# A Fourier-mix and attention kernel on Trainium2: products of zeros ahead of the first operands, and the first operands loaded, rounded and multiplied in another order

## The chip, the cores and the metric

The kernel runs on one core of one Trainium2 chip. The metric is the device time of one execution in microseconds (us). The kernel before takes 1727.77 us, the median of three runs (1727.48 to 1729.41).

The engines are named as the profile names them. PE multiplies matrices, and PEld is its load of the stationary operand. DVE is VectorE, ACT is ScalarE, POOL is GpSimd. SP is SyncE, which here only issues DMAs. SPq, ACTq and so on are the engines' instruction queues, where DMAs are issued.

## The reference

With x of 2048 rows and 512 columns, the kernel computes a gated sum of two branches:

```python
g = sigmoid((x * gate_w).sum(-1, keepdims=True))
# branch A: the real part of a DFT over columns, then rows
a, b = x @ Wd_re.T, x @ Wd_im.T
A = Ws_re @ a - Ws_im @ b
# branch B: attention, 32 heads of 16
q, k, v = split_heads(x @ wqkv)
B = (softmax(q @ k.T * 16 ** -0.5) @ v) @ wo
out = g * A + (1 - g) * B
```

All arrays are float32. The kernel writes each operand as a high part, rounded to the matrix engine's single-pass float format (fp32r in the profile), plus a low part, the remainder. A product of two operands is then three matrix products: high by high, low by high, high by low.

## The kernel before, in words

The kernel has two stretches. The first, about 200 us, makes q and k (the lines 127 to 187), v and the imaginary part of the column DFT (lines 286 to 342). The second, about 1500 us, weaves attention, the DFT over rows and the output projection into each other, in patterns written out by hand (lines 754 to 861). The order of instructions is fixed throughout: every engine and every DMA queue works its instructions in the order of the program, and each waits for its operands by semaphores.

The change touches the beginning and one small step near the end.

**The beginning.** x is held transposed: `xab[tb]` holds four blocks of 128 rows by 512 columns for the column block `tb` (512 of the 2048 positions), each as high and low part. `wh` and `wl` are the high and low parts of the weights of q (c = 0) and k (c = 1), in four parts `kt` of 128 input rows. `add` (line 98) puts a load on a list: first the weights of q and the x of `tb` 0, in turn for `kt` 0 to 3, so that load 0 is w of `kt` 0, load 1 is x of `kt` 0, load 2 is w of `kt` 1, load 3 is x of `kt` 1. Then come the weights of k, the x of `tb` 1 to 3, the weights of v and of the column DFT. `load_ahead` (line 101) issues loads of 256 KB each into one of six staging buffers `raw`, all from SP (line 95), five ahead. `split(n)` (line 106) takes n staged arrays in order. For each, `hi_lo` (line 74) rounds the high part on ACT (line 75) and subtracts it on DVE, for some on POOL (line 76), and the buffer is free for the next load.

`split(8)` (line 154) thus queues the rounding of all eight arrays of q's weights and the first x. The loop at line 173 then runs over `kt` and, within it, over the four tiles `ct` of 128 q rows. Each call of `mm_qk` issues the three products of one tile and one `kt` (lines 79 to 81): high by high, w high by x low, w low by x high. So four accumulators grow in turn, 48 products in all. Then `split(4)` queues the weights of k, and `evac_qk` (line 136) takes the four accumulators out, high part by ACT and low part by DVE, and SP writes them to memory. All other tiles of q and k are made one at a time, twelve products each, with one or two splits between a tile's products and its evacuation (lines 180 to 185). Their accumulators rotate through six banks, three named s and three named a.

**The step near the end.** The softmax denominators of four pairs of heads at a time are gathered into a tile `rc` of 128 rows by 64 (`sums`, line 476), inverted by DVE (`inverse`, line 484) and written back for a later multiplication. The last group of the second half of the rows has three pairs (n = 3), which leaves 32 of the 128 rows of `rc` unwritten, and there the inversion is done in two calls of 48 rows (line 491). `sums` and `inverse` of that group are placed by the plan at steps 482 and 484 of 512 (lines 721 to 726).

Of the kernel before, what the change touches and what calls it, by code (L numbers as in the profile page):

```python
# [9 lines left out]
F32 = mybir.dt.float32  # L10
F32R = mybir.dt.float32r
AF = mybir.ActivationFunctionType
ALU = mybir.AluOpType
AX = mybir.AxisListType

P = 128
# [5 lines left out]
KT = D // P  # L22
# [9 lines left out]
def mix_kernel(ctx: ExitStack, tc: tile.TileContext, xa_t, xa, wqkv, w_hid, w_seq, wo, gate_w, out):  # L32
# [5 lines left out]
    nc = tc.nc  # L38
# [5 lines left out]
    psD = ctx.enter_context(tc.tile_pool(name="psD", bufs=1, space=PSUM))  # L44
# [26 lines left out]
    xab = [const.tile([P, 4, 2, D], F32R, name=f"xab{tb}", tag=f"xab{tb}") for tb in range(4)]  # L71
    acc = psO.tile([P, 512], F32, name="acc")

    def hi_lo(hi, lo, src, lo_eng=None):
        nc.scalar.copy(hi, src)  # L75
        (lo_eng or nc.vector).tensor_tensor(lo, src, hi.bitcast(F32), ALU.subtract)

    def mm3(ps, sh, sl, mh, ml, first, last):
        nc.tensor.matmul(ps, sh, mh, start=first, stop=False)  # L79
        nc.tensor.matmul(ps, sh, ml, start=False, stop=False)  # L80
        nc.tensor.matmul(ps, sl, mh, start=False, stop=last)  # L81
# [8 lines left out]

    todo, loaded = [], []

    def staged(src):
        raw = st1.tile([P, D], F32, name="raw", bufs=RAW)
        nc.sync.dma_start(raw, src)
        return raw

    def add(hi, lo, src, lo_eng, shape=None):
        todo.append((hi, lo, src, lo_eng, shape))

    def load_ahead():
        while todo and len(loaded) < RAW - 1:
            hi, lo, src, lo_eng, shape = todo.pop(0)
            loaded.append((hi, lo, staged(src), lo_eng, shape))

    def split(n):

        for _ in range(n):
            load_ahead()
            if loaded:  # L110
                hi, lo, raw, lo_eng, shape = loaded.pop(0)
                hi_lo(hi, lo, raw.rearrange("p (s t) -> p s t", s=4) if shape else raw, lo_eng)
            load_ahead()

    def add_x(tb, kt):
        x = xab[tb][:, :, :, kt * P:(kt + 1) * P]
        add(x[:, :, 0], x[:, :, 1], xa_t[tb, :, kt], nc.vector, True)
# [3 lines left out]
    def bank():  # L121
        nonlocal banks
        banks += 1
        return (psS if banks % 2 else psA).tile([P, 512], F32, name="s" if banks % 2 else "a")


    with tc.tile_pool(name="qk", bufs=1, reuse_waits="tile") as pool:
        wh = pool.tile([P, 2, KT, D], F32R, name="wh")
        wl = pool.tile([P, 2, KT, D], F32R, name="wl")

        def mm_qk(ps, c, ct, tb, kt):
            cols = slice(ct * P, (ct + 1) * P)
            x = xab[tb][:, :, :, kt * P:(kt + 1) * P]
            mm3(ps, wh[:, c, kt, cols], wl[:, c, kt, cols], x[:, :, 0], x[:, :, 1], kt == 0, kt == KT - 1)

        def evac_qk(ps, c, ct, tb):
            hl = pool.tile([P, 2, D], F32R, name="hl", bufs=7)
            hi_lo(hl[:, 0], hl[:, 1], ps)
            nc.sync.dma_start(qk_d[c][:, ct * P:(ct + 1) * P, tb * 512:(tb + 1) * 512].rearrange("v p t -> p v t"),
                              hl.bitcast(F32))  # L140

        for kt in range(KT):
            add(wh[:, 0, kt], wl[:, 0, kt], wqkv[0, :, kt], nc.vector)
            add_x(0, kt)
        for kt in range(KT):
            add(wh[:, 1, kt], wl[:, 1, kt], wqkv[1, :, kt], nc.vector)
        for tb in range(1, 4):
            for kt in range(KT):
                add_x(tb, kt)
        for kt in range(KT):  # L150
            add(wv[0][kt], wv[1][kt], wqkv[2, :, kt], nc.gpsimd)
        for kt in range(KT):
            add(wch[:, kt], wcl[:, kt], w_hid[1, :, kt], nc.gpsimd)
        split(8)

        xgs = {}

        def gate_row(s):

            xg = xgs.pop(s)  # L160
            nc.vector.scalar_tensor_tensor(xg, xg, 1.0, gwb, op0=ALU.mult, op1=ALU.mult, accum_out=z[:, s:s + 1])
            if s + 5 < NT:
                xgs[s + 5] = staged(xa[s + 5])

        for tb in range(4):
            if tb == 2:
                assert not todo and not loaded
                nc.sync.dma_start(gwb, gate_w.broadcast_to([P, D]))
                xgs.update({s: staged(xa[s]) for s in range(5)})
            for c in range(2):  # L170
                if tb == 0 and c == 0:
                    pss = [bank() for _ in range(4)]
                    for kt in range(KT):
                        for ct in range(4):
                            mm_qk(pss[ct], c, ct, tb, kt)
                    split(4)
                    for ct in range(4):
                        evac_qk(pss[ct], c, ct, tb)
                    continue
                for ct in range(4):  # L180
                    ps = bank()
                    for kt in range(KT):
                        mm_qk(ps, c, ct, tb, kt)
                    split(1 if ct % 2 and tb else 2)
                    evac_qk(ps, c, ct, tb)
                    if tb > 1:
                        gate_row(8 * (tb - 2) + 4 * c + ct)
# [135 lines left out]
    for s in range(8):  # L323
        ps = psS.tile([P, 512], F32, name="s")
# [151 lines left out]
    def sums(hf, ct, n=4):  # L476

        rcs[hf, ct] = rc = work.tile([P, 64], F32, name="rc", bufs=2)
        for h in range(2):
            s0 = 32 if h else 16  # L480
            nc.sync.dma_start(rc[64 * h:64 * h + 16 * n],
                              o_d[hf][4 * ct:4 * ct + n, s0:s0 + 1].rearrange("p o (c f) -> (o c) p f", f=64))

    def inverse(hf, ct, n=4):
        rc = rcs.pop((hf, ct))
        if n == 4:
            nc.vector.reciprocal(rc, rc)
        for h in range(2):
            rows = rc[64 * h:64 * h + 16 * n]
            if n < 4:  # L490
                nc.vector.reciprocal(rows, rows)
            nc.sync.dma_start(r_d[hf][ct][h, :n].rearrange("p (c f) -> c p f", f=64), rows)

    def load_o(o, sm, hf, ct, q0, n=4):
# [226 lines left out]
    for hf in range(2):  # L721
        for ct in range(4):
            n = 3 if hf and ct == 3 else 4
            last = 32 * (4 * ct + n - 1) + 16 * (hf + 1)
            at(last + (4 if ct < 3 else 2), sums, hf, ct, n)
            at(last + (12 if ct < 3 else 4), inverse, hf, ct, n)
            if ct < 3:
                for half in range(2):
                    for step, du in enumerate((16, 20, 22)):
                        at(last + du + 8 * half, block, step, hf, ct, half)  # L730
# [167 lines left out]
```

## Time and profile before

| what | value |
|---|---|
| median of three runs | 1727.77 us |
| the profiled execution's own time | 1727.72 us |
| its span, from the first to the last instruction | 1725.9 us |
| time around the span | 1.8 us |
| PE busy | 1711.7 us (99% of the span), 13009 products |
| DVE busy | 1364.2 us (79%) |
| ACT busy | 1150.7 us (67%) |
| POOL busy | 447.3 us (26%) |

The busy share of PE is an upper bound: its products overlap, and their ends are modelled. What one product costs the chain is read from the distance between the starts of two products in a row. The page also shows the chain of work that ended last, followed back from the last instruction, and for each group of instructions the idle time before it with what ended it. In rows of the timeline the columns are the start in us, the duration in us, the engine, the line, the operation, output and inputs, the count, and in brackets the idle time before and what ended it. Rows of one line's instructions give the shortest, median and longest duration in ns.

### The profile page before, as it was taken

Reading aid. Unit: us, or ns where it says so; the run is one execution under the profiler, and the core shown is the slowest. Engines: PE = TensorE matmul, PEld = TensorE weight load, DVE = VectorE, ACT = ScalarE, POOL = GpSimd, SP = SyncE. Lnnn points to the kernel's source line nnn. Section 1 sums busy time; section 2 is a strip of 40 time slices with the busy share of each in tenths; the row PEclk is TensorE's granted clock in tenths of the full one; section 3 lists DMA queues with packets and bytes.
Section 4 is the critical chain, followed back from the end, with each engine's and each line's share of the span. In section 5 each row is a group of like instructions: output and inputs, shape, how many; then the busy total and the mean of one; then the engine's idle time right before and its main releaser. Section 6 shows DMA issues by size and latency. Waiting matters only on the chain.

```text
span 1725.9 us, 33460 instructions
## 1 busy us (share of the span) xinstructions
PE 1711.7 (99%) x13009; PEld 1049.2 (61%) x13009; DVE 1364.2 (79%) x2295; ACT 1150.7 (67%) x2257; POOL 447.3 (26%) x561
## 2 busy tenths in 40 slices
PE   8999999999999999999999999999999999999998
PEld 7888745456665666666656666666666666544443
DVE  5439788888888888888888888888888888899953
ACT  5212377776776777667776777677677777777776
POOL 0211122322222333222222343333232343200111
PEclk9999999999999999999999999999999999999999
DMA  8963500314141434314147535233142534560113
GB/s 284 335 150 134 155 7 3 55 35 78 56 75 45 84 98 96 72 38 81 38 93 246 104 106 107 63 64 67 45 86 63 124 99 94 177 151 18 39 28 129
DMA packets 82350, 164.82 MB, mean 95 GB/s; under 512 B 19712, under 2 KB 19968, under 8 KB 78352
## 3 DMA queue, kind: packets, MB, share of 16 engines
q1 hardware_dynamic: 77840, 162.30, 37.0%
q8 instruction: 102, 1.67, 0.4%
q0 software_dynamic: 4352, 0.39, 0.3%
q14 instruction: 56, 0.46, 0.1%
HBM read 107.47 MB, written 54.52 MB: 94 GB/s over the span
## 4 chain that ended last, share of the span: by engine, by line
PE 98%; ACT 1%; DVE 0%; DMA 0%; issue 0%; DVEq 0%; ACTq 0%
PE d L381 35%; PE acc L679 28%; PE a L216 12%; PE s L670 12%; PE s L295 3%; PE s L327 1%; PE d L295 1%; PE s L79 1%; PE s L80 1%; PE a L79 1%; PE a L80 1%; PE s L81 1%; PE a L81 1%; ACT pt L671 0%; PE a L381 0%; PE acc L216 0%
## 5 line engine op out<-in xcount | busy, mean ns | idle before, releaser
L218 DVE TENSOR_REDUCE mx<-a 128x1 f32<-128x512 f32 x2026 | 1245.8, 682 | 243.6 <-PE a L216 227.6
L671 ACT ACTIVATE pt<-s 128x512 f32<-128x512 f32 x2008 | 1024.2, 620 | 389.1 <-PE s L670 328.9
L216 PE MATMUL a<-ks,qs 48*128 48x512 f32 x2026 | 813.9, 416 | 0.7 <-DVE mx L218 0.7
L670 PE MATMUL s<-qs,ks 50*128 50x512 f32 x2008 | 769.7, 413 | 0.4 <-ACT pt L671 0.2
L381 PE MATMUL d<-xab,ch 64*128 64x512 f32 x2016 | 648.5, 396 | 0.0
L679 PE MATMUL acc<-pt,vt 128*17 128x512 f32 x4096 | 500.7, 596 | 0.0
L381 PEld LDWEIGHTS d<-xab,ch 64*128 64x128 f32 x2016 | 366.0, 184 | 126.0 <-DVE mx L218 60.4
L670 PEld LDWEIGHTS s<-qs,ks 50*128 50x128 f32 x2008 | 366.1, 184 | 110.0 <-ACT pt L671 32.4
L216 PEld LDWEIGHTS a<-ks,qs 48*128 48x128 f32 x2026 | 368.2, 185 | 67.3 <-DVE mx L218 40.6
L381 PE MATMUL d<-xab,cl 64*128 64x512 f32 x1008 | 399.4, 396 | 0.0
L381 PEld LDWEIGHTS d<-xab,cl 64*128 64x128 f32 x1008 | 185.5, 184 | 64.9 <-DVE mx L218 40.8
L365 POOL CAST ch<-craw 128x512 fp32r<-128x512 f32 x126 | 77.3, 614 | 555.5 <-PE d L381 205.6
L679 PEld LDWEIGHTS acc<-pt,vt 128*17 128x17 f32 x4096 | 90.6, 96 | 205.9 <-issue 205.8
L366 POOL TENSOR_TENSOR cl<-craw,ch 128x512 fp32r<-128x512 f32 x126 | 162.5, 1289 | 10.2
L239 POOL DMA_DIRECT2D qs<-mt x128 | 72.2, 569 | 157.8 <-DVE mt L235 149.6
L381 PE MATMUL d<-wre,xab 64*128 64x512 f32 (+1 forms) x348 | 93.8, 402 | 0.1
L381 PEld LDWEIGHTS d<-wre,xab 64*128 64x128 f32 (+1 forms) x348 | 60.0, 185 | 32.3 <-issue 23.6
L381 PE MATMUL d<-wo_hl,o_hl 64*128 64x512 f32 (+1 forms) x261 | 71.0, 397 | 0.0
L75 ACT CAST hl<-s 128x512 fp32r<-128x512 f32 x28 | 16.1, 587 | 62.9 <-PE s L295 31.2
L381 PEld LDWEIGHTS d<-wo_hl,o_hl 64*128 64x128 f32 (+1 forms) x261 | 47.2, 185 | 16.1 <-issue 11.7
L230 POOL CAST nhl<-nm 128x16 fp32r<-128x16 f32 x32 | 6.3, 197 | 161.6 <-DVE nm L227 161.6
L398 POOL CAST xab<-y 128x512 fp32r<-128x512 f32 x16 | 9.8, 612 | 129.7 <-ACT y L397 107.1
(132 smaller groups left out, 970.9 us busy)
## 6 DMA issues: line engine op xcount, KB each, us to landing
craw<-w_seq SPq DMA_DIRECT2D x128, 256.0 KB
qk<-hl SPq DMA_DIRECT2D x32, 512.0 KB
qs<-qk SPq DMA_DIRECT2D x96, 128.0 KB
ks<-qk SPq DMA_DIRECT2D x96, 128.0 KB
b<-hl SPq DMA_DIRECT2D x16, 512.0 KB
xab<-b SPq DMA_DIRECT2D x16, 512.0 KB
o<-oe SPq DMA_DIRECT2D x62, 128.0 KB
oh<-nh SPq DMA_DIRECT2D x12, 512.0 KB
```

Source lines behind the costliest of these rows:

```text
L79: nc.tensor.matmul(ps, sh, mh, start=first, stop=False)
L80: nc.tensor.matmul(ps, sh, ml, start=False, stop=False)
L216: nc.tensor.matmul(ps, qs[p % 2][r, qt * P:(qt + 1) * P], ks[p % 2][r, kb * 512:(kb + 1) * 512], start=True, stop=True)
L218: user = nc.vector.tensor_reduce(mx[p % 2][:, h, qt, kb:kb + 1], ps, AX.X, ALU.max)
L239: (nc.sync, nc.gpsimd)[h].dma_start(rows.rearrange("v (q b c) -> v b q c", q=8, b=4)[:, b], mt[hf][32 * b + h:32 * b + 32:2])
L295: i = nc.tensor.matmul(ps, st[r], mv[r], start=not half and not j, stop=half == 1 and j == 11)
L365: nc.gpsimd.tensor_copy(h1, raw)
L366: nc.gpsimd.tensor_tensor(l1, raw, h1.bitcast(F32), ALU.subtract)
L381: i = nc.tensor.matmul(self.ps, st[r], mv[r], start=not self.begun, stop=stop)
L670: nc.tensor.matmul(ps, ks[p % 2][rr, kt * P:(kt + 1) * P], qs[p % 2][rr, q0:q0 + 512], start=True, stop=True)
L671: return nc.scalar.activation(pts[u][:, 2 * qb + h], ps, AF.Exp, bias=0.0, scale=DH ** -0.5)
L679: nc.tensor.matmul(acc[32 * j:32 * j + 17], vt[:, kt, p, 16 * h:16 * h + 17], pt[:, j], start=kt == 0, stop=kt == NT - 1)
```

## The change

Five things are changed.

- `warm_up` fills the place of one later x block in `xab[3]` with zeros on DVE, and PE multiplies it by itself nine times into an accumulator that is not read. These nine products stand ahead of all other products.
- Loads 1 and 3, the first two x loads, are issued by ACT's queue and no longer by SP's.
- `split_first` does the first weights and the first x: ACT rounds w, DVE rounds x, then DVE makes both low parts. `split(8)` becomes `split(6)`.
- In the loop over `kt` the order inside one `kt` is by parts: the four tiles' products of high by high, then the four of w low by x high, then the four of w high by x low.
- In `sums` with n = 3, POOL fills `rc` with ones ahead of the gathering, and `inverse` inverts all 128 rows in one call, as the other groups do.

```diff
-    def staged(src):
+    def staged(src, queue=None):
         raw = st1.tile([P, D], F32, name="raw", bufs=RAW)
-        nc.sync.dma_start(raw, src)
+        (queue or nc.sync).dma_start(raw, src)
         return raw
...
+    loads = 0
+
     def load_ahead():
+        nonlocal loads
         while todo and len(loaded) < RAW - 1:
             hi, lo, src, lo_eng, shape = todo.pop(0)
-            loaded.append((hi, lo, staged(src), lo_eng, shape))
+
+            loaded.append((hi, lo, staged(src, nc.scalar if loads in (1, 3) else None), lo_eng, shape))
+            loads += 1
...
+    def split_first():
+
+        load_ahead()
+        (wh0, wl0, w_raw, _, _), (xh0, xl0, x_raw, _, _) = loaded.pop(0), loaded.pop(0)
+        x_raw = x_raw.rearrange("p (s t) -> p s t", s=4)
+        nc.scalar.copy(wh0, w_raw)
+        nc.vector.tensor_copy(xh0, x_raw)
+        nc.vector.tensor_tensor(wl0, w_raw, wh0.bitcast(F32), ALU.subtract)
+        nc.vector.tensor_tensor(xl0, x_raw, xh0.bitcast(F32), ALU.subtract)
+        load_ahead()
+
+    def warm_up():
+
+        zeros = xab[3][:, 0, 0]
+        nc.vector.memset(zeros.bitcast(F32), 0.0)
+        ps = psD.tile([P, 512], F32, name="d")
+        for i in range(9):
+            nc.tensor.matmul(ps, zeros[:, :P], zeros, start=True, stop=True)
...
-        split(8)
+        warm_up()
+        split_first()
+        split(6)
...
                     for kt in range(KT):
-                        for ct in range(4):
-                            mm_qk(pss[ct], c, ct, tb, kt)
+                        x = xab[tb][:, :, :, kt * P:(kt + 1) * P]
+                        for i, (w, v) in enumerate(((wh, 0), (wl, 0), (wh, 1))):
+                            for ct in range(4):
+                                nc.tensor.matmul(pss[ct], w[:, c, kt, ct * P:(ct + 1) * P], x[:, :, v],
+                                                 start=kt == 0 and i == 0, stop=kt == KT - 1 and i == 2)
...
         rcs[hf, ct] = rc = work.tile([P, 64], F32, name="rc", bufs=2)
+        if n < 4:
+            nc.gpsimd.memset(rc, 1.0)
...
         rc = rcs.pop((hf, ct))
-        if n == 4:
-            nc.vector.reciprocal(rc, rc)
+        nc.vector.reciprocal(rc, rc)
         for h in range(2):
             rows = rc[64 * h:64 * h + 16 * n]
-            if n < 4:
-                nc.vector.reciprocal(rows, rows)
             nc.sync.dma_start(r_d[hf][ct][h, :n].rearrange("p (c f) -> c p f", f=64), rows)
```

## The prediction

> **What bounds the kernel now.** I read the chain that ended last first, then the table of stages of the first 90 us, then the timeline of the first 20 us engine by engine, and last the places where the chain leaves PE.
>
> ```profile
> span 1725.9 us, 33460 instructions
> ...
> PE 98%; ACT 1%; DVE 0%; DMA 0%; issue 0%; DVEq 0%; ACTq 0%
> ```
>
> The chain is PE almost throughout, so what PE does earlier at the beginning is worth its full length, if nothing later holds it back. The stages (bounds and length in us, then busy us and count of PE, PEld, DVE, ACT and POOL, the granted clock, the DMA share and GB/s) split at the first product, at the thirteenth, at the first of the second weight matrix, and at 50:
>
> ```profile
> 5.78:11.36 5.58, 5.58 (x13) 4.09 (x13) 4.75 (x8) 3.71 (x6) 0.00 (x0) 1.00 0.88 289
> 11.36:19.54 8.18, 8.18 (x37) 6.76 (x36) 3.99 (x7) 4.14 (x7) 0.00 (x0) 1.00 0.66 211
> 19.54:50.00 30.46, 30.46 (x136) 25.23 (x135) 15.64 (x25) 16.12 (x31) 7.26 (x6) 1.00 1.04 338
> 50.00:90.00 40.00, 40.00 (x178) 33.14 (x177) 18.18 (x41) 9.79 (x17) 3.91 (x4) 1.00 0.96 322
> ```
>
> PE is never idle from 5.78 to 90. But of the 48 products of the first four tiles, 12 start in the first 5.58 us and 36 in the next 8.18, which is 0.227 each. The timeline shows why:
>
> ```profile
> 0.74 1.28 ACT L75 ACT_TABLE_LOAD   x1 [0.74 <-PEq L891]
> 0.75 0.39 SPq L95 DMA_DIRECT2D raw<-wqkv  x1
> 1.19 0.42 SPq L95 DMA_DIRECT2D raw<-xa_t  x1
> ...
> 4.47 0.62 ACT L75 CAST wh<-raw 128x512 fp32r<-128x512 f32 x1 [2.45 <-DMA raw<-wqkv]
> 5.11 0.62 ACT L75 CAST xab<-raw 128x512 fp32r<-128x512 f32 x1
> 5.12 0.69 DVE L76 TENSOR_TENSOR wl<-raw,wh 128x512 fp32r<-128x512 f32 x1 [5.12 <-ACT wh L75]
> 5.76 0.69 DVE L76 TENSOR_TENSOR xab<-raw,xab 128x512 fp32r<-128x512 f32 x1
> ...
> 5.78 0.80 PE L79 MATMUL s<-xab,wh 128*128 128x512 f32 x1 [5.78 <-ACT xab L75]
> ...
> 6.50 0.80 PE L80 MATMUL s<-xab,wh 128*128 128x512 f32 x1
> ...
> 7.09 0.63 PE L81 MATMUL s<-xab,wl 128*128 128x512 f32 x1
> ...
> 10.94 0.58 PE L81 MATMUL a<-xab,wl 128*128 128x512 f32 x1
> ...
> 11.36 0.39 PE L79 MATMUL s<-xab,wh 128*128 128x512 f32 x1
> ```
>
> From the third product (7.09) to the twelfth (10.94) the nine steps are 0.428 each; from 11.36 they are 0.227, with the same shapes and sources. That is PE at about half rate for its first 5.58 us. The granted clock reads 1.00 in both stages, so at the start that column does not show it; the distances do. Ahead of that PE waits for w, rounded by ACT, then for x, rounded by ACT after it; and the second product waits for x's low part (0.72 behind the first).
>
> **The change part by part.** *Clock.* The fill of zeros, the products behind it and the rounding of x on DVE have these nearest rows:
>
> ```profile
> L340 DVE MEMSET acc<- x1: 485/485/485, 197.1 to 197.1; 128x512 f32 x1
> ...
> L528 DVE CAST o_lno<-o_raw x1: 416/416/416, 1661.6 to 1661.6; 128x512 fp32r<-128x512 f32 x1
> ```
>
> DVE should start with the other engines at 0.74, so the zeros stand at 1.25 and PE starts at about 1.3. Nine products at 0.428 are 3.85 us: PE is done at 5.15 at the latest, ahead of the first operands. They cost nothing while that holds; each 0.1 us beyond the operands would cost 0.1. The first 12 real products then take 12 x 0.227 = 2.73 instead of 5.58, **2.85 less**. When the clock rises is bounded thus: at best before the operands come (no loss); at worst as late behind its first product as now, 5.58, that is at 6.9, so that 1.3 us of real products run at half rate and lose 0.47 of it, 0.6. I take 0.2, nearer to the first, because the 5.58 of now hold gaps that nine products in a row do not.
>
> *Start.* The first x goes by ACT's queue. If its issue stands ahead of the table load, it leaves at 0.74 instead of 1.19. But x and w then share the engines, and both of today's first two loads were there by 5.11: w lands between 4.47 and 5.11, x by 5.11. ACT's rounding of w (0.62) ends between 5.09 and 5.73, DVE's of x (0.42) by 5.53. The first product starts between 5.15 and 5.8; I take 5.6, nearer to the late end, since the same bytes must come. So the second queue and the second engine hardly move the start. The two issues on ACT, about 0.4 each by SP's rows, lie in the 2.45 us in which ACT waits; SP's other loads leave 0.46 or 0.93 earlier, behind the same bytes.
>
> *Low parts, order.* DVE makes w's low part at 5.75 to 6.44 and x's to 7.13. Four products of high by high from 5.6 end at 6.5, four more at 7.4: in the new order the low parts come in time, where now the second and third products waited. What is late next is `kt` 1:
>
> ```profile
> 5.84 0.33 SPq L95 DMA_DIRECT2D raw<-wqkv  x1
> 6.15 0.62 ACT L75 CAST wh<-raw 128x512 fp32r<-128x512 f32 x1 [0.43 <-DMA raw<-wqkv]
> ...
> 7.16 0.62 ACT L75 CAST xab<-raw 128x512 fp32r<-128x512 f32 x1 [0.39 <-DMA raw<-xa_t]
> ...
> 9.35 0.62 ACT L75 CAST wh<-raw 128x512 fp32r<-128x512 f32 x1 [0.23 <-DMA raw<-wqkv]
> ...
> 10.04 0.62 ACT L75 CAST xab<-raw 128x512 fp32r<-128x512 f32 x1
> ```
>
> Loads 2 and 3 share again, so I let both land at 7.16, today's landing of the second of them. ACT rounds w by 7.78 and x by 8.42; `kt` 1 can start at 8.47. `kt` 0 is done at 5.6 + 2.73 + 0.2 = 8.53. So the two meet, and the four tiles end at 8.53 + 8.18 = 16.71 against 19.54: **2.83**. The low parts of `kt` 1 (to 8.5 and 9.2) are wanted at 9.4 and 10.3.
>
> *What is queued behind.* Loads 6 and 7 (the w and x of `kt` 3) wait for the buffers that the first low parts free. They now leave at 6.44 and 7.13 instead of 5.84 and 6.47, so ACT's two rows at 9.35 and 10.04 move to about 10.0 and 10.7; the low part of x is there by 12.1, and PE wants `kt` 3 at 8.53 + 24 x 0.227 = 13.98. Covered by 1.9.
>
> *Does the gain survive?* From 19.54 to 90 the DMA engines are full (shares 1.04 and 0.96), and loads that are not early can hold ACT, behind which the evacuations stand:
>
> ```profile
> 27.48 0.39 PE L81 MATMUL s<-xab,wl 128*128 128x512 f32 x1
> ...
> 30.53 0.62 ACT L75 CAST xab<-raw 128x512 fp32r<-128x512 f32 x1 [4.24 <-DMA raw<-xa_t]
> 31.06 0.58 ACT L75 CAST hl<-s 128x512 fp32r<-128x512 f32 x1
> ```
>
> A tile whose last product starts at 27.48 is taken out at 31.06, since ACT waits 4.24 us for an x load. With PE 2.83 earlier and the loads not at all, that lag grows from 3.2 to 6.0, and with both halves of the evacuation (0.58 and 0.69) to 7.3. Six banks give five tiles of 12 x 0.227, 13.6 us. The cover holds, and everything behind is released by PE.
>
> *Reciprocals.* Here DVE is the bound for a moment:
>
> ```profile
> L491 DVE RECIPROCAL rc<-rc x2: 533/541/549, 1638.3 to 1638.9; 48x64 f32<-48x64 f32 x2
> ...
> L487 DVE RECIPROCAL rc<-rc x7: 506/508/552, 572.6 to 1680.6; 128x64 f32<-128x64 f32 x7
> ...
> 1638.37 0.45 DVE rc L491
> ...
> 1638.85 0.55 DVE rc L491
> ...
> 1640.18 0.50 PE L216 MATMUL a<-ks,qs 48*128 48x512 f32 x1 [0.69 <-DVE mx L218]
> ```
>
> Both calls stand in the chain (the third and fourth rows), and PE then waits 0.69 for DVE. One call of 0.51 in place of two, 1.08, frees **0.57**; the gain lies between nothing (if another wait takes its place) and 0.69. I take 0.57, because the wait is longer than what goes. The fill of ones runs on POOL:
>
> ```profile
> 1618.67 1.86 POOL L499 MEMSET o_raw<- 128x1024 f32 x2
> 1656.27 0.20 POOL L230 CAST nhl<-nm 128x16 fp32r<-128x16 f32 x1 [35.74 <-DVE nm L227]
> ```
>
> In program order it stands ahead of the first of these rows, under 0.93 by that row's mean for 16 times the elements, and POOL is idle for 35.74 behind them; it costs nothing. Without that cover SP's gathering would wait for it, and the inversion behind that.
>
> *Sum.* 2.83 + 0.57 = 3.40. Against the profiled execution's own 1727.72 (span 1725.9, 1.8 around it), 0.05 under the median shown: **1724.3**.
>
> **The rivals.** *The clock rises late* (1725.3). What counts may be a stretch of time that does not begin with the first product. The end of the trace has a hint:
>
> ```profile
> 1717.50:1718.00 0.50, 0.38 (x3) 0.06 (x1) 0.50 (x2) 0.22 (x1) 0.50 (x1) 1.00 0.29 107
> 1718.00:1718.50 0.50, 0.46 (x2) 0.46 (x4) 0.50 (x1) 0.47 (x1) 0.50 (x1) 0.51 0.56 217
> ```
>
> The clock falls to half at 1718.0 while products are still issued, so the decision has its own time. If it rises at 8.0, 2.4 us of real products lose 0.47 of it, 1.13: `kt` 0 ends at 9.46, the tiles at 17.64, 1.90 earlier, with the reciprocal 2.47. For it: now it took 5.58. Against: nine products fill 3.85 us without a gap. [...]
>
> *The products of zeros do not release the clock* (the change does not do what it says, 1726.5): the first 12 real products take 12 x 0.428 = 5.14 from 5.6, ending at 10.74, and the tiles end at 18.92, 0.62 earlier; with the reciprocal 1.19. Only that no product of zeros stands in this trace speaks for it.
>
> *x stands behind the table load* (1725.2): ACT issues it at 2.02. With the first load's 3.72 from issue to use it lands at 5.74, behind SP's loads as late as 7.16; in between, the first product starts at 6.7 and the tiles end at 17.6, 1.93 earlier. In the trace the table load is ACT's first instruction, but so is the activation behind it, so this stays open. [...]
>
> *More* (1723.7): x and w land early, the start is 5.15, `kt` 1 is ready at 7.8, and the head gives 3.48.
>
> *The reciprocal pays nothing* (1724.9): another wait of PE's or ACT's follows at once.
>
> *Slower* (1729.7): the second queue's first x waits behind full rings. The point from which it decides is a first product at 19.54 + 0.57 - 48 x 0.227 = 9.2, x landing at 8.75. Loads into full rings are that slow later on, as the tile of k's stacks shows:
>
> ```profile
> DMA to landing us min/median/max: 5.8/8.7/11.0
> ```
>
> From 2.02, 8.7 us give 10.7, a first product at 11.2 and tiles ending at 22.1, 2.56 later, less 0.57. Against it: at the start only three of SP's loads are in the rings.
>
> **How the numbers follow.** Chances: the forecast 0.50 (1723.9 to 1724.8), more 0.13, late clock 0.12, no clock 0.08, x behind the table load 0.08, no reciprocal 0.04, slower 0.05. The range 1723.2 to 1726.0 leaves out no clock and slower, and some of the edges. A measurement of this kernel can tell about 0.2%, 3.46 us, from no change, and the forecast, 3.4, sits right at that: half of its cases and all of "more" lie beyond. So faster by over 0.2% 0.43, within 0.2% 0.54, slower by over 0.2% 0.03.
>
> **What would show it.** Right: PE's first product of zeros at 1.3; distances of 0.227 from the first or second real product on; first product near 5.6; the first product of k's weights near 16.7; the later stages 2.8 earlier each, without a PE wait up to 90; one reciprocal at about 1635 and a PE wait near 0.1 behind it. Wrong: distances of 0.428 beyond 7; ACT's table load ahead of its DMA issues; a wait for `kt` 1 beyond 8.6; PE waits between 19 and 60.

## The result, and the profile after

The changed kernel takes 1725.33 us, the median of 20 executions (1724.36 to 1727.86). The kernel before, taken beside it in 20 executions, took 1728.43 (1727.15 to 1732.44). The ratio is 0.9982, with a 95% interval of 0.9976 to 0.9989: 0.18% or 3.10 us less, where 3.40 was forecast. As a time, 1725.33 is 1.03 above the 1724.3 of the forecast; 0.66 of that is that the kernel before came out at 1728.43 and not at the 1727.77 known when the forecast was made.

The profiled execution of the changed kernel is one of its longer ones: 1726.38, with a span of 1724.3, where the median span of the 20 is 1723.4. Against the profile before, the span is only 1.6 shorter. That a single pair of profiles differs from the medians shows how much varies from one execution to the next. These are the page's span and the shares of the chain:

```profile
span 1724.3 us, 33482 instructions
...
PE 98%; DVE 0%; DMA 0%; ACT 0%; issue 0%; POOL 0%; DVEq 0%; ACTq 0%; POOLq 0%
```

The table of stages (columns as before) at the first product of zeros, the first real product, the thirteenth and the first of k's weights:

```profile
1.46:5.61 4.15, 4.15 (x10) 2.87 (x10) 0.54 (x2) 1.90 (x2) 0.00 (x0) 1.00 0.84 272
5.61:9.19 3.58, 3.58 (x14) 2.89 (x13) 3.08 (x6) 2.18 (x4) 0.00 (x0) 1.00 0.74 258
9.19:17.35 8.16, 8.16 (x37) 6.76 (x36) 4.70 (x7) 4.21 (x7) 0.00 (x0) 1.00 0.86 280
```

The first 12 real products take 3.58 (5.58 before), the other 36 take 8.16 (8.18 before), and the first product of k's weights starts at 17.35 (19.54 before). The head has given 2.19. The timeline of the changed kernel's head:

```profile
0.74 0.90 ACTq L95 DMA_DIRECT2D raw<-xa_t  x2
0.75 1.34 SPq L95 DMA_DIRECT2D raw<-wqkv  x3
0.92 0.48 DVE L134 MEMSET xab<- 128x512 f32 x1 [0.92 <-PEq L919]
...
1.46 4.21 PE L137 MATMUL d<-xab 128*128 128x512 f32 x9 [1.46 <-DVE xab L134]
1.67 1.28 ACT L125 ACT_TABLE_LOAD   x1 [1.67 <-PEq L919]
...
4.84 0.62 ACT L125 CAST wh<-raw 128x512 fp32r<-128x512 f32 x1 [1.89 <-DMA raw<-wqkv]
5.03 0.43 DVE L126 CAST xab<-raw 128x512 fp32r<-128x512 f32 x1 [3.63 <-DMA raw<-xa_t]
...
5.61 0.77 PE L203 MATMUL s<-xab,wh 128*128 128x512 f32 x1
...
6.17 0.63 PE L203 MATMUL a<-xab,wh 128*128 128x512 f32 x1
...
6.63 0.62 ACT L75 CAST wh<-raw 128x512 fp32r<-128x512 f32 x1 [1.17 <-DMA raw<-wqkv]
...
7.03 0.47 PE L203 MATMUL a<-xab,wh 128*128 128x512 f32 x1
...
7.16 0.62 ACT L75 CAST xab<-raw 128x512 fp32r<-128x512 f32 x1
...
7.33 0.40 PE L203 MATMUL s<-xab,wl 128*128 128x512 f32 x1
```

ACT's two DMA issues stand ahead of its table load. The products of zeros run from 1.46. The first real product comes at 5.61, and only behind the fourth, between 7.03 and 7.33, do the distances fall from 0.43 to 0.23. The trace's own record of the clock begins with its rise, here at 7.17 and in the kernel before at 11.35; that is why the column of the granted clock read 1.00 from the start.

Matching the n-th exponential of ACT in one trace with the n-th in the other shows where the rest went. The changed kernel is 2.13 ahead when the second stretch starts (197), 1.79 ahead at 1452 by many small steps, only 0.55 ahead behind 1486, 1.32 behind 1641, and 1.60 behind 1680. The step at 1486 is one wait of PE's:

```profile
1478.88 2.57 SPq L494 DMA_DIRECT2D wo_hl<-wo  x4
...
1480.07 0.56 POOL L268 DMA_DIRECT2D qs<-mt  x1 [2.64 <-issue]
...
1485.34 0.47 PE L698 MATMUL s<-qs,ks 50*128 50x512 f32 x1 [1.23 <-DMA qs<-mt]
...
DMA to landing us min/median/max: 1.7/1.7/5.1
```

SP issues the load of the output projection's weights, four transfers of 512 KB. POOL issues the last of eight DMAs that put a pair's row maxima beside q; it moves 2 KB and lands 5.1 us later, where the median of its kind is 1.7 (the last line, from the tile of the maxima). In the kernel before the longest was 3.9, and PE did not wait:

```profile
DMA to landing us min/median/max: 1.7/1.7/3.9
```

The step near 1641 is the reciprocal:

```profile
1637.80 0.54 DVE L517 RECIPROCAL rc<-rc 128x64 f32<-128x64 f32 x1
...
1638.94 0.50 PE L245 MATMUL a<-ks,qs 48*128 48x512 f32 x1
```

One call stands where two stood, and the PE product that waited 0.69 for DVE has no wait any more.

### The profile page after: what moved, and what is told of

It is laid out like the page before. It is cut to its first block, busy times and chain, and to the rows that moved or that the text cites. A ratio compares the mean times of both kernels' runs of the same rounds, so it can differ in the third digit from the quotient of the medians.

```text
span 1724.3 us, 33482 instructions
## 1 busy us (share of the span) xinstructions
PE 1713.2 (99%) x13018; PEld 1043.1 (60%) x13018; DVE 1364.3 (79%) x2296; ACT 1149.4 (67%) x2256; POOL 446.5 (26%) x562
## 4 chain that ended last, share of the span: by engine, by line
PE 98%; DVE 0%; DMA 0%; ACT 0%; issue 0%; POOL 0%; DVEq 0%; ACTq 0%; POOLq 0%
PE d L410 35%; PE acc L707 28%; PE a L245 12%; PE s L698 12%; PE s L324 3%; PE s L356 1%; PE d L324 1%; PE a L81 1%; PE a L79 1%; PE s L81 1%; PE s L79 1%; PE a L80 1%; PE s L80 1%; PE a L410 0%; PE s L203 0%; PE a L203 0%
```

## The experiments

The theory to test was that all of the head's gain comes from the products of zeros, because they bring the clock up sooner (the clock theory). The rival was that the second queue, the rounding on two engines and the order by parts carry a good part (the operands theory). A second question was what sets the time of the rise. The executions of one kernel differ by more than the small terms (1724.36 to 1727.86 for the changed kernel), so these are read from the traces, and the times stand beside them. "Rest" below is the time from the first real product to the first of k's weights, less 48 products at the fast distance (8.16 / 36 each, from the stages above) and less 0.47 of the stretch at half rate (the share that a distance of 0.428 loses against 0.227): what PE waited in the head.

| run | first real product | clock rises | first of k's weights | rest |
|---|---|---|---|---|
| before | 5.78 | 11.35 | 19.54 | 0.27 |
| changed | 5.61 | 7.17 | 17.35 | 0.13 |
| b_warm | 5.81 | 4.49 | 17.32 | 0.63 |
| a_nowarm | 5.89 | 11.79 | 19.62 | 0.07 |
| b_recip | 5.55 | 10.20 | 18.88 | 0.26 |
| a_onequeue | 5.51 | 6.47 | 16.94 | 0.10 |
| a_again | 5.74 | 7.37 | 17.52 | 0.13 |
| a_four | 5.52 | 11.52 | 19.33 | 0.11 |
| a_order | 5.49 | 4.54 | 17.52 | 1.16 |
| a_late_wo | 5.46 | 4.29 | 16.46 | 0.12 |
| c_best | 5.49 | 6.12 | 16.74 | 0.07 |
| b_late_wo | 5.86 | 10.03 | 18.99 | 0.29 |
| c_z8 | 5.72 | 10.64 | 19.01 | 0.10 |
| c_z7 | 5.84 | 5.08 | 16.81 | 0.09 |

**The products of zeros alone (b_warm)**, added to the kernel before:

```diff
+        warm_up()
         split(8)
```

> The kernel before plus the fill of zeros and the nine products of zeros, nothing else. Clock theory (all that the head gains comes from the products of zeros): first product of zeros at about 1.5, half rate until about 7.1, the first product of k's weights at 17.4 instead of 19.54, and the time 2.1 lower. Operands theory (the second queue, the rounding on two engines and the order by parts carry a good part): the second and third real products still wait for the low parts, the first product of k's weights comes at 17.9 or later, and the time is 1.6 lower or less.

The first product of k's weights came at 17.32, as early as in the changed kernel. PE's rows of this run:

```profile
1.46 3.74 PE L121 MATMUL d<-xab 128*128 128x512 f32 x9 [1.46 <-DVE xab L118]
5.81 0.50 PE L79 MATMUL s<-xab,wh 128*128 128x512 f32 x1 [0.60 <-ACT xab L75]
6.53 0.50 PE L80 MATMUL s<-xab,wh 128*128 128x512 f32 x1 [0.23 <-DVE xab L76]
```

But it got there in another way than expected. The clock rose at 4.49, while the zeros were still running, so no real product ran at half rate, and 0.63 was lost to waiting for low parts. With the changed kernel's later rise it would have come about 0.6 later: (7.17 - 5.81) x 0.47. The time, 1726.68 against 1727.21 (ratio 0.9998, 0.9988 to 1.0007), does not show the 2.1 that the clock theory expected; the span's median over 10 executions is 1724.35 against 1725.4, half of it. In the trace the lead is 2.16 at the start of the second stretch and 1.80 near the end. Why the median of the spans shows less is not known; of the time, a longer part around the span takes some more (up to 2.79 here, at most 1.85 in the kernel before beside it).

**Everything but the products of zeros (a_nowarm)**:

```diff
-        warm_up()
         split_first()
```

> The changed kernel without the fill and the products of zeros. Clock theory: first product near 5.6, half rate for 5.6 us behind it, so to 11.2, and the first product of k's weights at 19.1, 0.4 earlier than in the kernel before; the time is 1.8 over the changed kernel. Operands theory: the first product of k's weights at 18.5 or earlier.

The first product of k's weights came at 19.62, no earlier than in the kernel before. The clock rose at 11.79:

```profile
11.58 0.50 PE L194 MATMUL a<-xab,wh 128*128 128x512 f32 x1
11.91 0.39 PE L194 MATMUL s<-xab,wh 128*128 128x512 f32 x1
12.14 0.39 PE L194 MATMUL a<-xab,wh 128*128 128x512 f32 x1
```

So without the zeros the other three parts of the head bring little, and the clock theory holds against its rival as put. They do save 0.2 of waiting even so (a rest of 0.07 against 0.27); that it does not show at 19.62 is chance, since here the clock rose 5.90 behind the first product and in the kernel before 5.57. The time was 1726.0 against 1727.21 (0.9993, 0.9983 to 1.0002), about what the reciprocal alone gives below.

**The reciprocal alone (b_recip)**, on the kernel before:

```diff
+        if n < 4:
+            nc.gpsimd.memset(rc, 1.0)
...
-        if n == 4:
-            nc.vector.reciprocal(rc, rc)
+        nc.vector.reciprocal(rc, rc)
...
-            if n < 4:
-                nc.vector.reciprocal(rows, rows)
```

> The kernel before with the one change at the reciprocal (ones into the tile on POOL, one call of 128 rows). If DVE is the bound there: PE's wait of 0.69 at 1640 goes and the steps behind it come 0.6 to 0.8 earlier relative to those ahead; the time is 0.6 to 0.8 lower. Rival (another wait follows at once): the steps behind 1650 come less than 0.2 earlier.

From the 1930th to the 1960th exponential of ACT it took 21.61, against 22.44 in all three kernels with the old one (before, b_warm, b_late_wo) and 21.61 to 21.63 in every other with the new one: 0.83 less, somewhat over the 0.6 to 0.8 expected. The time was 1726.2 against 1727.21 (0.9995, 0.9986 to 1.0005). The wait does not come back; another 0.3 is gained behind 1680 in every kernel with this change whose clock did not fall there, and its cause stays open. The profile of this run shows something else, in three stages of 3.41:

```profile
1655.43:1658.84 3.41, 3.19 (x15) 1.71 (x12) 0.43 (x2) 2.87 (x7) 2.91 (x4) 1.00 0.01 1
1658.84:1662.25 3.41, 3.41 (x11) 2.17 (x9) 0.56 (x1) 1.20 (x3) 2.07 (x4) 0.50 0.04 4
1662.25:1665.66 3.41, 3.41 (x27) 1.18 (x24) 2.25 (x5) 2.81 (x6) 0.00 (x0) 1.00 0.00 0
```

In the middle of the kernel the granted clock fell to 0.50 for 3.41 us, behind a stage with 15 products, and rose again. It cost this execution 1.8 in its last part (55.60 from the 1960th exponential to the last one, against 53.75). It begins 1648.64 behind the rise (10.20 to 1658.84); the fall at the end comes 1706.66 behind it in the kernel before (11.35 to 1718.01) and 1710.08 in the changed one (7.17 to 1717.25), and what sets these times is not shown. The trace of b_late_wo below has the same fall, at 1658.67: its granted clock is 0.93 in the mean from 1650 to 1660 and 0.89 from 1655 to 1670. The granted clock listed for single executions hints that it is not rare: both of these list 0.997, and so do 17 of the 31 executions of the kernel before that ran beside a_again, but only 1 of the 20 of the changed kernel and none of the 10 of a_again. Whether all these hold such a fall is not shown.

**All first loads on one queue (a_onequeue)**:

```diff
-            loaded.append((hi, lo, staged(src, nc.scalar if loads in (1, 3) else None), lo_eng, shape))
+            loaded.append((hi, lo, staged(src, None), lo_eng, shape))
```

> The changed kernel with all first loads on SP's queue. If the second queue brings nothing: w lands at 4.47 again and x by 5.1, x is rounded by 5.55, and the first real product starts at 5.6 as in the changed kernel, the first product of k's weights at 17.3 to 17.4. If the second queue does bring x earlier: the first real product starts at 5.9 or later.

The roundings of the first two arrays:

```profile
3.96 0.62 ACT L125 CAST wh<-raw 128x512 fp32r<-128x512 f32 x1 [1.93 <-DMA raw<-wqkv]
...
4.93 0.43 DVE L126 CAST xab<-raw 128x512 fp32r<-128x512 f32 x1 [3.53 <-DMA raw<-xa_t]
```

w came 0.88 earlier than with two queues (3.96 against 4.84), x 0.10 earlier (4.93 against 5.03), and the first real product started at 5.51 against 5.61. With the second queue w comes later and x no earlier, so it brings nothing. The first product of k's weights came at 16.94 and not at 17.3, because the clock rose at 6.47. This kernel ran once, in 1724.9. In all runs the first product lies between 5.46 and 5.89 with two queues and between 5.49 and 5.86 with one.

**The changed kernel once more (a_again)**, without an edit:

> The changed kernel once more, unchanged, to see what varies between executions. [...] Delay theory (a fixed time behind the first product): the rise comes at 7.0 to 7.2 again. PE's wait for the DMA of the maxima's rows near 1484 is anything from 0 to 1.3.

The rise came at 7.37 instead of 7.17, and PE waited 0.7 near 1484. The time was 1725.47 against 1728.1 (0.9985, 0.9976 to 0.9994). This run alone does not speak against the delay theory, for 5.91 behind the first product of zeros is near the 5.71 of the first profile. The others do: with nine products from 1.46 the rise came at 4.29, 4.49, 4.54, 6.47, 7.17 and 7.37, that is 2.83 to 5.91 behind the first. The delay theory falls; what sets the rise within that spread is not shown.

**Four products (a_four)**:

```diff
-        for i in range(9):
+        for i in range(4):
```

> The changed kernel with four products of zeros instead of nine; they end at about 3.4, and PE is idle for 2.2 us until the first operands. [...] Rival (what counts is the sum of work since the start): the rise between 7.2 and 8.2, and the first product of k's weights by 17.7.

The rise came at 11.52 and the first product of k's weights at 19.33, so four products are as good as none. PE stood idle in front of the first real product, by the list of waits:

```profile
PE s L203 <- ACT wh L125: 2.0, 1, 2.0
```

It is not work summed up that counts: behind the idle 2.0 the rise came 6.00 after the first real product, about as late as without any zeros (5.57 in the kernel before, 5.90 in a_nowarm), and the rival, which had it by 8.2, falls. The time was 1727.55, 2.1 over a_again on the same chip, against 1.8 in the head.

**The old order inside a part (a_order)**:

```diff
-                        x = xab[tb][:, :, :, kt * P:(kt + 1) * P]
-                        for i, (w, v) in enumerate(((wh, 0), (wl, 0), (wh, 1))):
-                            for ct in range(4):
-                                nc.tensor.matmul(pss[ct], w[:, c, kt, ct * P:(ct + 1) * P], x[:, :, v],
-                                                 start=kt == 0 and i == 0, stop=kt == KT - 1 and i == 2)
+                        for ct in range(4):
+                            mm_qk(pss[ct], c, ct, tb, kt)
```

> The changed kernel with the old order inside each part kt, so that the second product wants the low part of x at once. The time from the first real product to the first of k's weights, less 48 products of 0.227 and less 0.47 of the stretch at half rate, is what PE waits: 0.13 in the changed kernel, 0.63 in the kernel before with the products of zeros. If the order by parts is what makes the difference: 0.5 to 0.8 here. If the rounding on two engines makes it: 0.2 or less.

The second product wants the low part of x, which DVE now makes after the high part of x and the low part of w:

```profile
5.49 0.47 PE L79 MATMUL s<-xab,wh 128*128 128x512 f32 x1 [0.27 <-ACT wh L125]
6.73 0.50 PE L80 MATMUL s<-xab,wh 128*128 128x512 f32 x1 [0.78 <-DVE xab L128]
```

The rest is 1.16, more than expected and more than the 0.63 of the old rounding with the old order. So once the clock is early and the rounding is shared, the order by parts is worth about 1.0, and the shared rounding without it loses 0.5. What the order is worth with the old rounding was not run. A part of the operands theory comes back here: these parts are worth 0.2 without the zeros and 0.5 beside them (0.63 in b_warm against 0.12). The time was 1726.41 against 1728.1 (0.9993, 0.9983 to 1.0003), 0.9 over a_again on the same chip.

**The later load (a_late_wo)**, a further edit on the changed kernel:

```diff
-            end_tiles(s // 4)
+            for i in ([], [0, 1], [2], [3])[s // 4]:
+                end_tiles(i)
```

> The changed kernel with the load of the output projection's weights (four of 512 KB on SP's queue, from 1478.9) issued one step later, together with the next loads near 1491; they are first used at 1507. If this transfer is what holds up the last DMA of the maxima's rows on POOL's queue: that DMA lands in about 1.7 us, PE's wait of 1.2 near 1484 is gone in every profile, and the time is 0.5 to 1.0 lower than the changed kernel's. Rival (that DMA is late by itself, by the 2.6 us that POOL stops ahead of issuing it): the wait stays between 0 and 1.3.

PE did not wait near 1484, and the longest landing of its kind was:

```profile
DMA to landing us min/median/max: 1.7/1.7/2.8
```

The DMA that had taken 5.1 took 1.69, though POOL stopped for 2.63 ahead of it as before; the rival falls. So it is in every trace: that DMA takes 1.69 to 1.73 in the five with the later load (c_best, c_z8 and c_z7 below among them) and 3.84 to 5.20 in the nine without. The time was 1724.47 against 1728.1 (0.9981, 0.9972 to 0.9991), 1.0 under a_again on the same chip. The same edit on the kernel before:

> The kernel before with the later load of the output projection's weights alone. If the wait for the DMA of the maxima's rows strikes the kernel before as often as the changed one, the time is 0.4 to 0.8 lower; if it strikes only the changed kernel, no change.

The time was 1727.57 against 1728.1 (0.9997, 0.9988 to 1.0006), and its profile has no such wait, but the fall of the clock near 1660 instead. By the time this is inconclusive. That the wait strikes kernels with the old head too is shown by b_recip, where it was 1.3.

**The best version (c_best)**, with the later load, one queue, and earlier and longer zeros:

```diff
-        zeros = xab[3][:, 0, 0]
+        zeros = xab[3][:, 0, 0, :P]
...
-        for i in range(9):
-            nc.tensor.matmul(ps, zeros[:, :P], zeros, start=True, stop=True)
+        for i in range(10):
+            nc.tensor.matmul(ps, zeros, zeros.rearrange("p (a b) -> p a b", a=1).broadcast_to([P, 4, P]), start=True, stop=True)
```

> The changed kernel with three edits: all first loads on SP's queue; the zeros filled over 128 columns instead of 512, read four times by each of now ten products; the load of the output projection's weights issued one step later. [...] The time is 3.5 to 4.5 under the kernel before, about that of the changed kernel with the late load or up to 0.3 lower.

PE started at 1.06, and the clock rose at 6.12. The spans of its 11 executions lie between 1722.1 and 1723.4, their median 1722.5 against 1726.3 before. The time was 1724.55 against 1728.1 (0.9981, 0.9972 to 0.9990). By its median it is under the kernel before and the changed one, but not under a_late_wo, which ran on another chip. The time gained 3.55 where the span gained 3.8, since the time around the span was 1.74 to 3.80 in this kernel. One line of the DMA table for the last 11 us of its profile, an execution with 2.9 around its span, is not there in the kernel before:

```profile
q8 instruction: 1, 0.02, 0.8%
```

One more block of instructions is fetched at the very end (103 in the trace instead of 102), and it starts at 1724.33, behind the span of 1722.6. To see whether fewer PE instructions avoid it, the same kernel ran with eight and with seven products:

```diff
-        for i in range(10):
+        for i in range(8):
```

> The kernel with the three further edits (one queue for the first loads, zeros over 128 columns, the late load of the projection's weights) with eight products of zeros instead of ten. Instruction theory (the time around the span grows to as much as 3.8 where the added PE instructions, two for each product, make one more block of instructions be fetched at the very end): eight products are 16 instructions, less than the 18 of the kernels in which it grew and more than the 8 of the one in which it did not, so it may go either way. [...]

> The same with seven products of zeros (14 instructions). Instruction theory: nearer to the 8 instructions that cost nothing, the time around the span 1.73 to 1.86 in every run, and the time 0.3 or so lower than with ten products, if the clock still rises in time. [...] Rival (the longer time around the span comes with the early clock and not with instructions): it is as scattered here as with ten.

The time around the span was 1.72 to 2.11 with eight and 1.73 to 2.84 with seven, and both profiles have the 103rd fetch. So the expectation that seven products cost nothing fell. In all, the time around the span is 1.73 to 1.86 in every execution with at most four products and up to 3.80 with seven or more. That it is the fetch is suspected, not shown: the four profiles with the 103rd fetch (b_warm, c_best, c_z8, c_z7) have 1.9 to 2.9 around their spans, but the profile of the changed kernel has 102 fetches and 2.1. The rival, that it goes with the early clock, is not shown either: three of the six executions with the longer span in c_z8, in which the clock seems to have risen late, have 1.89 to 1.99. The clock rose at 5.08 in the profile with seven products and only at 10.64 in the one with eight. The spans fall into two groups, 1722.2 to 1722.3 and 1724.0 to 1724.3 with eight, 1722.0 to 1722.4 and 1724.2 to 1724.9 with seven. The times were 1725.88 (0.9984, 0.9975 to 0.9993) and 1724.83 (0.9985, 0.9976 to 0.9994), each against 1727.42. Ten products, from 1.06, show no second group of spans in 11 executions.

## Why the prediction was right, and where it was off

The direction and the main mechanism were right: PE runs at about half rate at its start (distances of 0.43 against 0.23), products of zeros move that stretch ahead of the operands, and the gain passes through to the end. Step by step:

- *Zeros from 1.3, done by 5.15, ahead of the operands.* They ran from 1.46, since DVE started at 0.92 and not 0.74, and the last started at 5.03. The cover held but was thinner than thought.
- *The start, 5.6.* 5.61. That the second queue and the second engine hardly move it was right, and a_onequeue shows it for the queue. For the engine no run changes it alone; over all traces the first real product lies at 5.55 to 5.86 with x rounded by ACT and at 5.46 to 5.89 with x rounded by DVE.
- *The clock, 0.2, at worst 0.6.* This is the term that was mis-sized. Real products ran at half rate from 5.61 to 7.17 and lost 0.73, beyond the stated worst case. That bound, "as late behind its first product as now", took one execution's delay for a limit. The delay behind the first product of zeros was 2.83 to 5.91 in the nine-product runs. The rival "late clock" had the time of the rise rightly free of the first product, but it was kept as a separate case when it is a spread within every case. Its rise at 8.0 was the author's estimate and no run with nine products shows it; they showed 4.29 to 7.37.
- *`kt` 1 ready at 8.47.* It was ready at 7.78, since w had landed by 6.63 and x by 7.16, and ACT rounded each at once. It held nothing up.
- *The head, 2.83.* 2.19 in the first pair of profiles. The head before moves with its rise too: its first product of k's weights lay at 18.88, 18.99 and 19.54 in three traces, with the rise at 10.20, 10.03 and 11.35. The low parts came in time, as forecast, because of the order by parts.
- *The gain survives 20 to 90.* It did: PE has no wait there in the changed kernel.
- *The reciprocal, 0.57.* 0.83, and 0.3 behind it, so it was beyond the 0.69 given as its most. The distance between the product that waited and the one ahead of it fell from 1.08 (1639.10 to 1640.18 in the kernel before) to 0.35 (1638.59 to 1638.94), which is 0.73; where the last 0.1 and the later 0.3 come from stays open.
- *Nothing behind that.* The forecast had no term for the 1.2 at 1485. The profile before had a hint: the same DMA landed in 3.9 against a median of 1.7, just in time.
- *The chances.* Half of the forecast and all of "more" are 0.38, and not the 0.43 given for faster by over 0.2%; the prediction says nothing of the rest.

That the medians' 3.10 is near the forecast's 3.40 is thus partly luck: in the traces a head that gave less and a reciprocal that gave more offset each other. The time of 1725.33 alone would have fitted "late clock" (1725.3), and in its mechanism the first profile is between the two: the clock rose at 7.17, the forecast's worst case being 6.9 and the rival's 8.0. If the fall of the clock near 1660 strikes the kernel before more often, as the lists hint, a part of the 3.10 comes from there; this stays open. The interval of the ratio, 0.9976 to 0.9989, leaves out no change, though the gain is under the 0.2% that the prediction wanted for telling the two apart.

## What to carry to other kernels

Where the first products wait for loads, look at the distances between their starts, not at the clock column: if they halve some microseconds in (from 0.43 to 0.23 here), fill PE's idle time from its earliest start to the first operands without a gap. With a pause of 0.9, in the profile of c_z8, the clock rose only at 10.64, and with one of 2.0, in a_four, at 11.52, about as late as without any products of zeros (10.03 to 11.79). With the clock up early, the order of the first products by the arrival of their operands pays more: together with the shared rounding 0.5 here, against 0.2 with the clock late. Look also for DMAs of a few KB whose landing is far over their median: here one of them, issued behind 2 MB that nobody needed yet, cost up to 1.3 us in some executions, and moving the 2 MB cost nothing.

## What was not expected of the hardware

- Products of zeros raise the clock as products of data do: the rise came at 4.29 to 7.37 with nine of them from 1.46, and at 10.03 to 11.79 with none.
- The rise keeps no fixed delay behind the first product of zeros: 2.83 to 5.91 us in six runs with nine of them from 1.46. What sets it within that spread is not shown.
- The clock fell in the middle of the kernel though PE was busy, by the profile, for 3.19 of the 3.41 us ahead of the fall (b_recip at 1658.84, in which it stayed at 0.50 for 3.41 us). The 15 products there were spread, and eight of them use 50 of the 128 rows; why it fell stays open.
- The time around the span was 1.73 to 1.86 with up to four products of zeros and up to 3.80 with seven or more. A last fetch of instructions is suspected; what causes it is not shown.
